# One attention-plus-rational-MLP kernel: scores in two 64-row halves of the array, a new task order, and 19 instead of 15 weight chunks converted in attention

## The chip, the core and the metric

The kernel runs on one core of one Trainium2 chip. The metric is the device time of one execution in microseconds (us). Each core has five engines that run their own instruction queues in order: PE (the matrix engine, with its weight loads shown as PEld), DVE (vector), ACT (scalar), POOL and SP. SP computes nothing here; it issues all the DMAs, in program order.

## The reference, cut to what matters

```python
# q, k, v: (4 batches, 12 heads, 448 tokens, 64) float32
scores = np.matmul(q, k.transpose(0, 1, 3, 2)) / 8.0
scores = np.where(np.triu(ones, k=1), -1e9, scores)        # causal
attn = np.exp(scores - scores.max(-1)); attn /= attn.sum(-1) + 1e-9
x = np.matmul(attn, v)                  # heads side by side: (1792, 768)
h = x @ w_in                            # w_in (768, 2048) float64
g = (a0 + a1*h + a2*h**2 + a3*h**3) / (1 + abs(b0)*abs(h) + abs(b1)*h**2 + 1e-6)
out = (g @ w_out).astype(np.float32)    # w_out (2048, 768) float64
```

## The kernel before, in words

**Attention** works on 24 pairs of heads (p = 0 to 23, `NP`). For a pair, q and k are loaded with one DMA for each head (`stage_load`, task `ld`), transposed on PE (`q`, `k`), and split into a high fp32r part on ACT (`qh`, `kh`) and the remainder on DVE (`ql`, `kl`). Scores (`s.i`, `stage_b_pe`) come in seven blocks of 64 queries. The stationary operand is `QH[p % 2][:, i]`: 128 columns, of which the first 64 hold head 0's queries in the upper 64 rows and the last 64 hold head 1's in the lower 64 rows, with zeros elsewhere. So a single matmul over all 128 rows gives both heads' scores, 64 output partitions each, over (i + 1) * 64 keys. Each block takes three passes (high times high, high times low, low times high); the two narrowest blocks do the first two in one instruction and add the result on DVE (`b`). DVE adds the mask and takes the row maximum (`m`), ACT takes the exponential (`e`), DVE the reciprocal of the sum (`r`), POOL multiplies (`n`). PE transposes the result in 16 pieces of 128 by 128, four to a PSUM tile (`c.0` to `c.3`). ACT (`a`) or DVE (`v`) copy these to SBUF. Four steps of plain fp32 matmuls multiply by v (`d.0` to `d.3`, `stage_d`), head 0 into output partitions 0 to 63 and head 1 into 64 to 127. For `d.3` the contraction has only 64 rows. ACT copies the result (`de`), and POOL splits it into `xh` and `xl` (`dh`, `dl`).

**Weight conversion.** The weights arrive as float64. A chunk (128 rows or columns of one weight, 768 KB) is turned into float32 by four steps (`conv_step`): step 0 on POOL for the first `NC` chunks and on ACT for the later ones, steps 1 to 3 on DVE (L146, L148, L153). The float32 chunk is stored to DRAM (`conv_store`, L159) and loaded again later (`load_w`, L172) into one of three buffers with the tag `ld`. There are 32 chunks. In attention, `cv.0` issues the POOL steps of a pair, `cv.1` and `cv.2` its DVE steps and `cv.3` the stores and the next loads. `quota(p)` is the number of DVE steps for a pair: three for the first two pairs, then two and one by turns, 39 in all, which is 13 chunks. Two more (13 and 14) are converted in `TAIL`, the other 17 in the MLP.

**Order.** `ORDER` is a list of tasks run for every pair p from 3 on; `@2` makes a task work on pair p - 2, `@-1` on pair p + 1. `HEAD` is a hand-over list for the first three pairs, `TAIL` the one that leads from the last pair into the MLP. The lists fix the order of the instructions on every engine and of the DMAs on SP.

**MLP.** 64 units t (4 token chunks of 512, 512, 384, 384 by 16 slices of the hidden width). `p1(t)` is 18 matmuls (L206), then ACT and DVE evaluate the rational function, and `p2(t)` is 24 or 18 matmuls (L520, L521). While the first token chunk is processed, the remaining 17 weight chunks are converted, one in each of t = 2 to 14 and a second one in t = 6, 8, 10 and 12 (`step`). `split_w` makes the high part on ACT (`w_hi`, L181) and the low part on POOL or DVE (`w_lo`, L189). At pair 22 four converted weights are loaded again, the fourth of which needs the buffer of the first to be free.

Of the kernel before, what the change touches and what calls it, by code (L numbers as in the profile page):

```python
# [24 lines left out]
NHEAD = 3  # L25
HEAD = """

ld@0 ab0 q@0 qh.0@0 xd.0 k@0 kh@0 ld@1 ql.0@0 qh.1@0 kl@0 xd.1 ql.1@0 s.1@0 s.0@0 s.2@0 b.1@0 b.0@0 m.0@0 q@1
m.1@0 e.0@0 cv.0@0 cv.1@0 qh.1@1 k@1 m.2@0 e.1@0 e.2@0 s.3@0 qh.0@1 ld@2 cv.2@0 s.6@0 s.4@0 ql.1@1 m.3@0 kh@1
e.3@0 kl@1 ql.0@1 s.5@0 m.6@0 e.6@0 m.5@0 cv.3@0 s.0@1 k@2 m.4@0 e.5@0 cv.0@1 cv.1@1 b.0@1 s.1@1 b.1@1 e.4@0  # L30
s.2@1 m.0@1 r@0 m.1@1 q@2 wh.0.0 n.4@0 e.0@1 n.1@0 s.6@1 m.2@1 e.1@1 e.2@1 n.0@0 n.5@0 qh.0@2 n.3@0 s.3@1 kh@2
n.6@0 qh.1@2 n.2@0 cv.2@1 m.6@1 ql.1@2 c.1@0 s.4@1 s.5@1 kl@2 a.1@0 m.3@1 e.6@1 ql.0@2 lv@0 c.0@0 m.5@1 e.3@1
s.1@2 ld@3 e.5@1 m.4@1 c.3@0 v.0@0 s.0@2 k@3 q@3 e.4@1 b.1@2 cv.3@1 r@1 cv.0@2 b.0@2 a.3@0 m.0@2 s.6@2 c.2@0
d.0@0 s.2@2 d.3@0 wl.0.0 m.1@2 cv.1@2 n.5@1 v.2@0 kh@3 wh.1.0 e.1@2 qh.1@3 e.0@2 d.1@0 m.2@2 m.6@2 s.3@2 kl@3
d.2@0 cv.2@2 n.2@1 n.4@1 m.3@2 n.6@1 n.0@1 n.1@1 e.6@2 c.1@1 cv.3@2 ld@4 s.4@2 qh.0@3 ql.1@3 s.5@2 lv@1 wl.1.0
# [13 lines left out]
def kernel(  # L49
# [11 lines left out]
    nc = tc.nc  # L61
# [15 lines left out]
    NC = 15  # L77
    NWB = (2, 3)
    NAB = 2
# [8 lines left out]
    mask = const.tile([P, S], F32, name="mask")  # L88
# [28 lines left out]
    def conv_load(m):  # L117
# [3 lines left out]
        early = m < NC or m % 2 == 0  # L121
# [11 lines left out]
    def conv_step(m, s):  # L133
# [9 lines left out]
        elif s == 1:  # L143
            pool = cv if m < NC or m % 2 == 0 else rp
# [71 lines left out]
    def stage_load(p):  # L216
        b, hp = divmod(p, HP)
        ts = {}
        for nm, src in (("q", q), ("k", k)):
            t = ld.tile([CP, NB, 2, D], F32, tag=nm, name=f"{nm}raw")  # L220
            for j in range(2):
                nc.sync.dma_start(
                    out=t[:, :, j], in_=src[b, 2 * hp + j].rearrange("(c p) d -> p c d", p=CP)
                )
            ts[nm] = t
        raw[p] = ts

    def stage_load_v(p):
        b, hp = divmod(p, HP)
        t = lv.tile([P, 2, 4, D], F32, tag="v", name="vraw")  # L230
# [7 lines left out]
        raw[p]["v"] = t  # L238


    def stage_a_pe(p, which):
        t = raw[p][which]
        ps = psa[p, which] = ps_t.tile([P, 512], F32, tag="t", name="psA")
        for c in range(NB):
            nc.tensor.transpose(  # L245
                ps[:, c * CP:(c + 1) * CP], t[:, c].rearrange("p j d -> p (j d)"), ident[:CP, :CP]
            )
# [4 lines left out]
    def q_pe(p):  # L252
        stage_a_pe(p, "q")


    def q_hi(p, j):
        nc.scalar.activation(
            out=QH[p % 2][half(j), :, j, :],
            in_=psa[p, "q"][half(j), :S].rearrange("d (i t) -> d i t", t=QB), func=AF.Copy, scale=SCALE,
        )  # L260

    def q_lo(p, j):
# [18 lines left out]

    def stage_b_pe(p, i):
        ps, w = ps_s.tile([P, 512], F32, tag="s", name="psS"), (i + 1) * QB
        pss[p, i] = ps
        qh, ql = (t[p % 2][:, i].rearrange("d j t -> d (j t)") for t in (QH, QL))
        if i < NAB:
            nc.tensor.matmul(
                ps[:, :2 * w].rearrange("m (x n) -> m x n", x=2), qh, K[p][:, :, :w], start=True, stop=True
            )
            nc.tensor.matmul(ps[:, :w], ql, K[p][:, 0, :w], start=False, stop=True, skip_group_check=True)  # L290
        else:
            for n, (a, b) in enumerate(((qh, 0), (qh, 1), (ql, 0))):
# [19 lines left out]
    def stage_b_exp(p, i):  # L312
        w = (i + 1) * QB
# [11 lines left out]
    def stage_b_norm(p, i):  # L325
        e = E[p % 2][i][:, :(i + 1) * QB]
# [5 lines left out]
    c_blocks = (  # L332
        [(0, 0), (0, 1), (0, 2), (0, 3)], [(0, 4), (0, 5), (0, 6), (3, 6)],
        [(1, 2), (1, 3), (1, 4), (1, 5)], [(1, 6), (2, 4), (2, 5), (2, 6)],
    )
    c_slot = (0, 8, 13, 7)

    def c_pe(p, n):
        ps = psc[p, n] = ps_t.tile([P, 512], F32, tag="t", name="psC")
        for o, (c, i) in enumerate(c_blocks[n]):  # L340
            nc.tensor.transpose(  # L341
                ps[:, o * P:(o + 1) * P], E[p % 2][i][:, c * P:(c + 1) * P], ident
            )
# [349 lines left out]
```

## Time and profile before

| what | value |
|---|---|
| time, three runs | 701.64 us median (701.62 to 702.39) |
| the profiled execution | 703.33 us, of which 701.6 us span from the first to the last instruction |
| granted PE clock, mean | 0.987 |
| busy, share of the span | PE 664.6 us (95%), DVE 541.1 (77%), ACT 441.0 (63%), POOL 198.7 (28%) |
| DMA | 161.98 MB, 231 GB/s, 72.4% of 16 engines |

Busy is the time in which an engine had at least one instruction in flight; ends of matmuls are modelled, so a PE that is busy all the time can still have gaps in its columns. The chain that ended last is 75% PE and 14% DVE.

### The profile page before, as it was taken

Reading aid. Unit: us, or ns where it says so; the run is one execution under the profiler, and the core shown is the slowest. Engines: PE = TensorE matmul, PEld = TensorE weight load, DVE = VectorE, ACT = ScalarE, POOL = GpSimd, SP = SyncE. Lnnn points to the kernel's source line nnn. Section 1 sums busy time; section 2 is a strip of 40 time slices with the busy share of each in tenths; the row PEclk is TensorE's granted clock in tenths of the full one; section 3 lists DMA queues with packets and bytes.
Section 4 is the critical chain, followed back from the end, with each engine's and each line's share of the span. In section 5 each row is a group of like instructions: output and inputs, shape, how many; then the busy total and the mean of one; then the engine's idle time right before and its main releaser. Section 6 shows DMA issues by size and latency. Waiting matters only on the chain.

```text
span 701.6 us, 11446 instructions
## 1 busy us (share of the span) xinstructions
PE 664.6 (95%) x3912; PEld 566.8 (81%) x3912; DVE 541.1 (77%) x1123; ACT 441.0 (63%) x962; POOL 198.7 (28%) x277
## 2 busy tenths in 40 slices
PE   5899999999968999888899999999999999999997
PEld 4687787787746787766688888888999999999996
DVE  4899999999829999999987766666566655666554
ACT  3789989989824676766567655554554454645543
POOL 4777887887837322122120000000000000000000
PEclk9999999999989999999999999999999999999999
DMA  8976788876433999887589766666877777877762
GB/s 195 214 161 147 178 191 183 170 162 147 149 113 108 358 349 346 284 268 253 191 316 359 275 226 242 247 220 214 282 273 254 257 244 257 304 264 241 255 225 112
DMA packets 110042, 161.98 MB, mean 231 GB/s; under 512 B 71072, under 2 KB 83360, under 8 KB 109984
## 3 DMA queue, kind: packets, MB, share of 16 engines
q1 hardware_dynamic: 109984, 161.25, 72.4%
q8 instruction: 31, 0.51, 0.3%
q14 instruction: 27, 0.22, 0.1%
HBM read 117.97 MB, written 43.25 MB: 230 GB/s over the span
## 4 chain that ended last, share of the span: by engine, by line
PE 75%; DVE 14%; issue 3%; DMA 3%; POOL 2%; ACT 1%; SPq 0%; DVEq 0%; POOLq 0%; ACTq 0%
PE psH L206 25%; PE psO L520 17%; PE psM L521 9%; PE psD L363 7%; PE psS L293 7%; PE psC L341 6%; PE psA L245 2%; DVE u L146 2%; DVE u L148 2%; DVE w L452 1%; DVE whl L189 1%; DVE p L483 1%; DVE p L460 1%; DMA raw<-in_moe_w_out_dram 1%; DVE p L477 1%
## 5 line engine op out<-in xcount | busy, mean ns | idle before, releaser
L206 PE MATMUL psH<-xh,whl 128*128 128x512 f32 (+1 forms) x768 | 177.7, 367 | 6.6 <-DVE p L460 6.6
L520 PE MATMUL psO<-whl,gh 128*128 128x512 f32 x448 | 160.3, 394 | 1.6 <-ACT gh L489 1.5
L206 PEld LDWEIGHTS psH<-xh,whl 128*128 128x128 f32 x768 | 136.5, 189 | 24.0 <-DVE p L460 5.5
L521 PE MATMUL psM<-whl,gh 128*128 128x256 f32 x448 | 126.2, 282 | 0.0
L327 POOL TENSOR_SCALAR e<-e,r 128x320 f32<-128x320 f32 (+6 forms) x168 | 94.2, 580 | 37.8 <-DVE nm L307 27.3
L467 ACT ACTIVATE u<-w,lnb 128x512 f32<-128x512 f32 (+1 forms) x64 | 43.0, 672 | 95.9 <-DVE w L452 95.9
L520 PEld LDWEIGHTS psO<-whl,gh 128*128 128x128 f32 x448 | 84.0, 187 | 22.1 <-ACT gh L489 5.1
L314 ACT ACTIVATE e<-psS,nm 128x64 f32<-128x64 f32 (+6 forms) x168 | 78.9, 474 | 23.1 <-DVE nm L307 20.4
L206 PE MATMUL psH<-xl,whl 128*128 128x512 f32 (+1 forms) x384 | 89.7, 369 | 0.0
L520 PE MATMUL psO<-whl,gl 128*128 128x512 f32 x224 | 81.2, 392 | 5.7 <-DVE gl L496 5.7
L496 DVE TENSOR_TENSOR gl<-p,gh 128x384 fp32r<-128x384 f32 (+1 forms) x62 | 38.4, 620 | 61.5 <-ACT gh L489 61.5
L521 PEld LDWEIGHTS psM<-whl,gh 128*128 128x128 f32 x448 | 84.5, 189 | 0.9
L206 PEld LDWEIGHTS psH<-xl,whl 128*128 128x128 f32 x384 | 71.8, 192 | 8.3
L445 ACT ACTIVATE u<-psH 128x512 f32<-128x512 f32 (+1 forms) x64 | 34.5, 538 | 69.1 <-PE psH L206 69.1
L521 PE MATMUL psM<-whl,gl 128*128 128x256 f32 x224 | 63.1, 282 | 0.0
L307 DVE CUSTOM_DVE_ANT_0 psS<-psS,mask 128x192 f32<-128x192 f32 (+4 forms) x120 | 56.9, 504 | 7.4 <-PE psS L293 7.2
L363 PE MATMUL psD<-at,vraw 128*64 128x448 f32 (+3 forms) x384 | 56.1, 408 | 6.7 <-DMA vraw<-in_v_dram 6.7
L293 PE MATMUL psS<-khl,qh 128*128 128x448 f32 (+4 forms) x240 | 60.8, 339 | 0.1
L341 PE MATMUL psC<-ident,e 128*128 128x128 f32 x384 | 56.1, 279 | 2.7 <-POOL e L327 2.7
L520 PEld LDWEIGHTS psO<-whl,gl 128*128 128x128 f32 x224 | 42.0, 188 | 15.4 <-DVE gl L496 6.7
L341 PEld LDWEIGHTS psC<-ident,e 128*128 128x128 f32 x384 | 43.1, 142 | 10.2 <-POOL e L327 5.7
L363 PEld LDWEIGHTS psD<-at,vraw 128*64 128x64 f32 (+1 forms) x384 | 21.6, 137 | 35.5 <-issue 24.3
(67 smaller groups left out, 1210.8 us busy)
## 6 DMA issues: line engine op xcount, KB each, us to landing
whl<-whl SPq DMA_DIRECT2D x112, 768.0 KB, 4.3
w<-w SPq DMA_DIRECT2D x34, 384.0 KB, 6.3
raw<-in_moe_w_in_dram SPq DMA_DIRECT2D x16, 768.0 KB, 6.2
w<-u SPq DMA_DIRECT2D x32, 384.0 KB, 2.8
raw<-in_moe_w_out_dram SPq DMA_DIRECT2D x16, 768.0 KB, 5.4
qraw<-in_q_dram SPq DMA_DIRECT2D x48, 112.0 KB, 4.7
kraw<-in_k_dram SPq DMA_DIRECT2D x48, 112.0 KB, 4.7
out_dram<-osb SPq DMA_DIRECT2D x14, 384.0 KB, 3.1
```

Source lines behind the costliest of these rows:

```text
L206: nc.tensor.matmul(ps, w[:, c * P:(c + 1) * P], x[c][:, lo:lo + n_tok], start=(c == 0 and n == 0), stop=(c == KD - 1 and n == 2),)
L293: nc.tensor.matmul(ps[:, :w], a, K[p][:, b, :w], start=(n == 0), stop=(n == 2))
L307: nc.vector.tensor_tensor_reduce(out=s, in0=s, in1=msk[p, i] if i < NAB else mask[:, S - w:], scale=-1.0, scalar=3e38, op0=ALU.add, op1=AL ...
L314: nc.scalar.activation(out=E[p % 2][i][:, :w], in_=pss[p, i][:, :w], func=AF.Exp, bias=nmx[p][:, i:i + 1], scale=-1.0, accum_out=SUM[p][:, ...
L327: nc.gpsimd.tensor_scalar(out=e, in0=e, scalar1=REC[p][:, i:i + 1], scalar2=0.0, op0=ALU.mult, op1=ALU.add)
L341: nc.tensor.transpose(ps[:, o * P:(o + 1) * P], E[p % 2][i][:, c * P:(c + 1) * P], ident)
L363: nc.tensor.matmul(ps[half(j), c * P:S], vt[:kk, j, c], AT[p][:kk, c_slot[c]:c_slot[c] + n, half(j)], start=(c == 0), stop=(c == 2), skip_ ...
L445: nc.scalar.activation(out=u, in_=h, func=AF.Abs)
L467: nc.scalar.activation(out=r, in_=w, func=AF.Ln, scale=2.0 ** -LSH, bias=lnb[:, 0:1])
L496: eng.tensor_tensor(out=gl, in0=pp, in1=gh.bitcast(F32), op=ALU.subtract)
L520: nc.tensor.matmul(acc[k], g, w[:, :512], start=first, stop=last)
L521: nc.tensor.matmul(m, g, w[:, 512:], start=first and k % 2 == 0, stop=last, skip_group_check=True)
```

## The change

Scores are taken in blocks of 128 queries. For the first 384 queries, head 0's operands lie in rows 0 to 63 and head 1's in rows 64 to 127, without zeros, and each head has its own matmul on its half of the rows, into its own PSUM bank. The last 64 queries keep the old form, with zeros (tile `Q6`, filled by DMA, zeroed once on POOL). There are seven row blocks with 128, 128, 256, 256, 384, 384 and 448 keys. The separate add of the narrow blocks is gone, `q_hi` and `q_lo` are one instruction each, q takes four DMAs instead of two, and `d.3` contracts over 128 rows (the unused ones zero). The tile for v is allocated once. The attention loop now starts at p = -2 with the ordinary order, and `HEAD` only loads. The order and the tail are new. `quota` is three steps for the first nine pairs and two for the others, 57 in all, which is 19 chunks; none is left for the tail, and 13 for the MLP, one in each of t = 2 to 14. The reload buffers (`ld` of `cv`) are four instead of three.

```diff
 ORDER = """
+e.0 m.1 m.2 e.1 v.0@2 cv.3 k@-1 n.0@1 ld@-2 n.4@1 m.3 lv@1 e.2 n.3@1 n.6@1 s.3 cv.2@-1 qh@-1 a.3@2 kh@-1 s.2
+n.2@1 n.1@1 d.0@2 e.3 m.6 m.4 d.3@2 n.5@1 e.6 m.5 e.4 ql@-1 d.1@2 d.2@2 cv.0@-2 de@2 c.2@1 e.5 kl@-1 c.1@1 dh@3
+cv.1@-2 s.0@-1 s.1@-1 a.2@1 c.0@1 m.0@-1 c.3@1 q@-2 r a.1@1 dl@3
 """
-NHEAD = 3
+NHEAD = -2
 HEAD = """
+ld@0 ab0 xd.0 ld@1 xd.1
 """
 TAIL = """
+v.0@2 n.0@1 n.4@1 lv@1 xr n.3@1 n.6@1 p1.0 wh.2.0 a.3@2 n.2@1 n.1@1 d.0@2 d.3@2 n.5@1 aa.0 d.1@2 d.2@2 xd.21 da.0
+de@2 c.2@1 c.1@1 dz.0 ab.0 dh@3 a.2@1 c.0@1 c.3@1 a.1@1 dl@3 p1.1 dh@2 aa.1 v.0@1 a.3@1 d.0@1 d.3@1 d.1@1 d.2@1 db.0 dy.0
+wl.2.0 lw.4.0 dl@2 da.1 gh.0 de@1 wh.0.1 p1.2 xl gl.0 dh@1 wl.0.1 dz.1 ab.1 wh.1.1 wh.3.0 xd.20 xd.22
+lw.2.1 wl.1.1 x.19.0 p2.0 lw.3.1 aa.2 lw.5.0 db.1 wl.3.0 dl@1 dy.1 wh.4.0 wl.4.0
 """
-    NC = 15
+    NC = 19
-            w = cv.tile([P, DM], F32, tag="ld", bufs=3, name="w")
+            w = cv.tile([P, DM], F32, tag="ld", bufs=4, name="w")
     def stage_load(p):
+        t = raw[p]["q"] = ld.tile([P, 3, 2, D], F32, tag="q", name="qraw")
+        for j in range(2):
+            src = q[b, 2 * hp + j]
+            nc.sync.dma_start(out=t[:, :, j], in_=src[:3 * P].rearrange("(c p) d -> p c d", p=P))
+            nc.sync.dma_start(out=Q6[p % 2][:, j, j], in_=src[3 * P:])
     def q_pe(p):
+        for c in range(3):
+            nc.tensor.transpose(
+                ps[:, c * P:(c + 1) * P], raw[p]["q"][:, c].rearrange("p j d -> p (j d)"), ident
+            )
+        for j in range(2):
+            nc.tensor.transpose(
+                ps[:, 3 * P + j * QB:3 * P + (j + 1) * QB], Q6[p % 2][:, j].rearrange("p j d -> p (j d)"),
+                ident[:QB, :QB],
+            )
     def stage_b_pe(p, i):
+        w = b_w[2 * i]
+        ps = [ps_s.tile([P, 512], F32, tag="s", name="psS") for _ in range(2 if i < 3 else 1)]
...
+        for n, (a, b) in enumerate(((QH, 0), (QH, 1), (QL, 0))):
+            for j in range(len(ps)):
+                d = half(j) if i < 3 else slice(None)
+                nc.tensor.matmul(
+                    ps[j][:, :w], a[p % 2][d, i * P:(i + 1) * P], K[p][d, b, :w],
+                    start=(n == 0), stop=(n == 2), skip_group_check=True,
+                )
-    def stage_b_add(p, i):
     def stage_d(p, c):
-                vt[:kk, j, c],
-                AT[p][:kk, c_slot[c]:c_slot[c] + n, half(j)],
+                ps[half(j), c * P:S], V[p % 2][:, j, c], AT[p, h][:, j, lo:lo + S - c * P],
     def quota(p):
-        return 3 if p < 2 else 2 - p % 2
+        return 3 if p < 9 else 2
         for p in range(NHEAD, NP):
+            if p in (0, 1):
+                split_w(p, 0)
-        step = {t: [todo.pop(0) for _ in range(1 + (t in (6, 8, 10, 12))) if todo] for t in range(2, NU)}
+        step = {t: [todo.pop(0) for _ in range(1) if todo] for t in range(2, NU)}
```

## Rows read from the trace of the kernel before

**Rows 1.** Windows: start:end, length, busy us of each engine, granted clock, DMA share, GB/s.

```profile
100.00:115.02 15.02, 15.02 (x122) 12.01 (x118) 14.12 (x49) 13.60 (x43) 12.08 (x20) 1.00 0.75 172
...
200.00:220.00 20.00, 14.83 (x77) 9.54 (x78) 9.87 (x14) 7.30 (x12) 8.40 (x9) 0.83 0.36 102
...
280.00:300.00 20.00, 17.32 (x85) 13.93 (x84) 19.93 (x26) 12.84 (x19) 4.14 (x2) 1.00 0.84 291
...
400.00:420.00 20.00, 20.00 (x105) 17.20 (x104) 12.37 (x18) 12.17 (x19) 0.00 (x0) 1.00 0.64 234
```

**Rows 2.** Chain that ended last, one pair: start us, us, engine, tile, line.

```profile
107.08 2.18 PE psD L363 x16
...
109.85 1.32 PE psS L293 x9
111.17 0.87 PE psC L341 x8
...
112.82 0.43 PE psA L245 x4
...
114.59 1.58 PE psD L363 x9
```

**Rows 3.** Groups by form on DVE, 40 to 180 us: busy us, mean ns | idle.

```profile
L263 DVE SCALAR_TENSOR_TENSOR ql<-psA,qh 64x448 fp32r<-64x448 f32 x38 | 23.6, 620 | 0.6
...
L153 DVE SCALAR_TENSOR_TENSOR u<-raw,u 128x768 uint32<-128x768 uint32 x10 | 12.5, 1248 | 0.0
L307 DVE CUSTOM_DVE_ANT_0 psS<-psS,mask 128x448 f32<-128x448 f32 x19 | 11.8, 620 | 0.0
...
L148 DVE SCALAR_TENSOR_TENSOR u<-raw,u 128x768 uint32<-128x768 uint32 x9 | 11.0, 1217 | 0.0
...
L307 DVE CUSTOM_DVE_ANT_0 psS<-psS,mask 128x256 f32<-128x256 f32 x19 | 8.2, 433 | 3.8 <-PE psS L293 3.7
...
L298 DVE TENSOR_TENSOR msk<-psS,mask 128x128 f32<-128x128 f32 x18 | 4.9, 273 | 0.0
L146 DVE TENSOR_SCALAR u<-raw 128x768 uint32<-128x768 uint32 x9 | 4.9, 543 | 0.0
...
L298 DVE TENSOR_TENSOR msk<-psS,mask 128x64 f32<-128x64 f32 x18 | 3.7, 207 | 0.0
```

**Rows 4.** Timeline of POOL and PE, start-up: start us, us, engine, line, instruction.

```profile
10.53 0.88 POOL L140 TENSOR_SCALAR raw<-raw 128x768 f32<-128x768 f32 x1 [3.29 <-DMA raw<-in_moe_w_in_dram]
...
30.56 0.97 PE L363 MATMUL psD<-at,vraw 128*64 128x448 f32 x4
...
39.46 2.25 PE L363 MATMUL psD<-at,vraw 128*64 128x448 f32 x16
```

**Rows 5.** From attention to MLP: timeline of PE and DVE, then chain.

```profile
188.83 2.25 PE L363 MATMUL psD<-at,vraw 128*64 128x448 f32 x16
...
196.91 1.52 PE L206 MATMUL psH<-xh,whl 128*128 128x512 f32 x6
205.17 4.12 PE L363 MATMUL psD<-at,vraw 128*64 128x448 f32 x16 [6.74 <-DMA vraw<-in_v_dram]
...
239.39 1.53 PE L206 MATMUL psH<-xh,whl 128*128 128x512 f32 x6
...
218.73 3.40 DVE L146 TENSOR_SCALAR u<-raw 128x768 uint32<-128x768 uint32 x2
...
201.22 0.32 SPq L172
...
201.63 3.40 DMA vraw<-in_v_dram
...
222.66 6.77 DMA raw<-in_moe_w_out_dram
```

**Rows 6.** Timeline of PE: first six matmuls of p1(8), p1(9), p1(10).

```profile
272.70 1.66 PE L206 MATMUL psH<-xh,whl 128*128 128x512 f32 x6
...
284.30 1.65 PE L206 MATMUL psH<-xh,whl 128*128 128x512 f32 x6 [0.73 <-DVE p L460]
...
292.98 1.56 PE L206 MATMUL psH<-xh,whl 128*128 128x512 f32 x6
```

More of the change, by code (lines that the diff above doesn't have):

```diff
@@ L87 @@
     ident = const.tile([P, P], F32, name="ident")
-    mask = const.tile([P, S], F32, name="mask")
+    mask = const.tile([P, 3 * P + S], F32, name="mask")
     ab = const.tile([P, 6], F32, name="ab")
@@ L216, in stage_load @@
     def stage_load(p):
+        if p in raw:
+            return
         b, hp = divmod(p, HP)
[L218 to L226, printed above, removed]
+        raw[p] = {}
+        t = raw[p]["q"] = ld.tile([P, 3, 2, D], F32, tag="q", name="qraw")
[3 more added lines that the diff above has]
+            nc.sync.dma_start(out=Q6[p % 2][:, j, j], in_=src[3 * P:])
+        t = raw[p]["k"] = ld.tile([CP, NB, 2, D], F32, tag="k", name="kraw")
+        for j in range(2):
+            nc.sync.dma_start(
+                out=t[:, :, j], in_=k[b, 2 * hp + j].rearrange("(c p) d -> p c d", p=CP)
+            )
     def stage_load_v(p):
         b, hp = divmod(p, HP)
-        t = lv.tile([P, 2, 4, D], F32, tag="v", name="vraw")
+        t = V[p % 2]
         for j in range(2):
@@ L237, in stage_load_v @@
         )
[L238 to L247, printed above, removed]
     def half(j):
@@ L252, in q_pe, with q_hi, q_lo @@
     def q_pe(p):
[L253 to L262, printed above, removed]
+        ps = psa[p, "q"] = ps_t.tile([P, 512], F32, tag="t", name="psA")
+        for c in range(3):
+            nc.tensor.transpose(
+                ps[:, c * P:(c + 1) * P], raw[p]["q"][:, c].rearrange("p j d -> p (j d)"), ident
+            )
+        for j in range(2):
+            nc.tensor.transpose(
+                ps[:, 3 * P + j * QB:3 * P + (j + 1) * QB], Q6[p % 2][:, j].rearrange("p j d -> p (j d)"),
+                ident[:QB, :QB],
+            )
+    def q_hi(p):
+        nc.scalar.activation(out=QH[p % 2], in_=psa[p, "q"], func=AF.Copy, scale=SCALE)
+    def q_lo(p):
         nc.vector.scalar_tensor_tensor(
-            out=QL[p % 2][half(j), :, j, :],
-            in0=psa[p, "q"][half(j), :S].rearrange("d (i t) -> d i t", t=QB), scalar=SCALE,
-            in1=QH[p % 2][half(j), :, j, :].bitcast(F32), op0=ALU.mult, op1=ALU.subtract,
+            out=QL[p % 2], in0=psa[p, "q"], scalar=SCALE, in1=QH[p % 2].bitcast(F32),
+            op0=ALU.mult, op1=ALU.subtract,
         )
     def k_pe(p):
-        stage_a_pe(p, "k")
+        ps = psa[p, "k"] = ps_t.tile([P, 512], F32, tag="t", name="psA")
+        for c in range(NB):
+            nc.tensor.transpose(
+                ps[:, c * CP:(c + 1) * CP], raw[p]["k"][:, c].rearrange("p j d -> p (j d)"), ident[:CP, :CP]
+            )
     def k_hi(p):
@@ L329, in stage_b_norm @@
         )
[L332 to L334 removed]
+    c_parts = (
+        [(0, 0, 0), (P, 0, 1)], [(0, 0, 2), (P, 0, 3), (P + QB, 3, 3)],
+        [(0, 1, 1), (P, 1, 2)], [(0, 1, 3), (QB, 2, 2), (QB + P, 2, 3)],
     )
[L336 removed]
+    c_of = {0: (0, 0), 3: (0, S), 1: (1, 0), 2: (1, S - P)}
     def c_pe(p, n):
[L339 to L343, printed above, removed]
+        ps = psc[p, n] = ps_t.tile([P, 2, 256], F32, tag="t", name="psC")
+        for o, c, i in c_parts[n]:
+            keys = slice(c * P, (c + 1) * P)
+            if i == 3:
+                nc.tensor.transpose(
+                    ps[:, :, o:o + QB], E[p % 2][6][:, keys], ident.rearrange("p (j t) -> p j t", j=2)
+                )
+            else:
+                for j in range(2):
+                    nc.tensor.transpose(ps[:, j, o:o + P], E[p % 2][2 * i + j][:, keys], ident)
     def c_ev(p, n, eng):
[L346 to L348 removed]
+        h = n // 2
+        if (p, h) not in AT:
+            AT[p, h] = at.tile([P, 2, 512], F32, tag=f"at{h}", name="at")
+        o = AT[p, h][:, :, (n % 2) * 256:(n % 2 + 1) * 256]
         ps = psc.pop((p, n))
```

90 lines of the change are left out of this document (33 added, 57 removed).

## The prediction

> **What bounds the kernel now.** I read the windows first, then the chain, then the groups by form and timelines. The windows [rows 1] show four regimes. In attention PE is busy 15.02 of 15.02 us at clock 1.00, with DVE at 14.12 close behind, then ACT 13.60 and POOL 12.08. At 200 to 220 no engine is full: PE has 14.83 of 20 and the clock drops to 0.83. At 280 to 300 DVE is full (19.93) and PE has room. From 400 on PE is full again and stays so to the end.
>
> The chain [rows 2] confirms the first: from one pair's first v matmul (107.08) to the next's (114.59) it holds PE pieces alone. A pair costs 7.51 us and PE sets it. DVE's 7.06 us a pair (14.12 / 2) is the next limit. In the transition [rows 5] PE does p1(0) until 198.43, then waits 6.74 us until 205.17 for a v tile. The chain names the cause: the v DMA starts right behind a DMA of L172 at 201.22, the fourth weight reload, which finds three buffers taken and holds SP's queue until POOL has finished with the first. A second transfer, raw chunk 15, starts late at 222.66 and takes 6.77 us, with ACT standing in front of it. DVE also does leftover conversion there (218.73). In the DVE-bound stretch [rows 6], p1(9) follows p1(8) by 11.6 us and p1(10) follows p1(9) by 8.7: the units after a doubled conversion are the long ones.
>
> **PE in attention.** Rates from [rows 2]: nine score passes of 256, 384 and 320 columns take 1.32 us, 0.458 ns a column, so 0.117, 0.176 and (448) 0.205 us a pass. Eight 128-column transposes take 0.87, 0.109 each; a score pass of 192 columns or fewer I price at the same 0.11, because its 128-column weight load is as long. Scores before: 3 x (0.205 + 0.176 + 0.147 + 0.117 + 0.11) + 4 x 0.11 = 2.70 us. After, if the two halves of the rows run at the same time, each pair of passes costs one: 3 x (0.11 + 0.117 + 0.176) + 3 x 0.205 = 1.82. Gain 0.88. If they run one after the other, 6 x 0.403 + 0.615 = 3.03, a loss of 0.33.
>
> No row shows two halves of the rows. The nearest is the v step: 16 fp32 instructions into two halves of the columns take 2.18 us [rows 2], while their 4,096 columns at the transposes' 0.85 ns (also fp32) would take 3.48 in sequence and 1.74 in parallel. So column halves do overlap, and I take the parallel price for row halves.
>
> The rest, 2.18 - 1.74 = 0.44 us, belongs to four changes of the array's shape in that step (to 128 by 64, to 64 by 64 for d.3, back, and out): 0.11 each. The change takes d.3's two away, but adds entry and exit: full to row halves (s.2), to column halves (d), to full (c.2), to row halves (s.0, s.1), to full (c.0), to row halves (the two 64-row transposes of q), to full. Seven instead of four: +0.33; bounds 0 (if row halves switch free) and 0.33. The transposes of q go from four of 112 (0.43) to five: 5 x 0.109 = 0.55, +0.12. Sum: 7.51 - 0.88 + 0.33 + 0.12 = 7.08.
>
> The Trainium skill, "TensorEngine Tiling (Array Packing)", section Key Properties, says that changing the tiling mode drains the engine, which speaks against a change that adds modes; the 0.11 us that the trace gives agrees. "TensorE: Matmul & The Clock Gate", Part 3, Measured speedup vs the span model, gives 3.07x for four row tiles; scaled to two tiles, an estimate of 1.53x, the three blocks would cost 2.42 / 1.53 = 1.58 instead of 1.21 us, and the whole time would be 680.
>
> **DVE in attention** [rows 3]. The adds go (0.273 + 0.207 = 0.48). Two ql of 0.620 become one of 512 columns, about 0.69: -0.55. The maxima get 192 more columns at (620 - 433) / 192 = 0.97 ns: +0.19. A chunk's three steps cost 0.543 + 1.217 + 1.248 = 3.01 us, 1.00 a step; 1.5 steps a pair become 3 and then 2. So 7.06 - 0.84 + 1.5 = 7.72 early and 7.06 - 0.84 + 0.5 = 6.72 later. Early pairs are then bound by DVE, later ones by PE. With some friction I take 7.8 and 7.2. The loop runs pair p's steps one or two iterations ahead, so six intervals between first v matmuls are early (pairs 0 to 6) and fourteen late.
>
> Edits at nothing: ACT has 6.80 us a pair, loses half a microsecond with one qh instead of two, and gains wider exponentials; POOL has 6.04 [rows 1], gains 0.5 at most for one POOL step every pair and 0.2 to 0.7 for wider products. Both lie under 7.8; if POOL's worst came, the late pairs would wait at most some 0.1 us. The two more q DMAs a pair carry no more bytes. DMA share is 0.75 over 7.51 us, 5.6 us a pair with half a chunk (0.58 MB of 1.29). Another half costs 2.5 us at the pair's mean rate, or 1.7 at the rate of 280 to 300 (291 GB/s at share 0.84): 7.3 to 8.1. At the upper end, six early pairs lose 0.3 each. The row masks, memsets and v tile are under POOL's start.
>
> **Start-up.** The plain order puts three DVE steps of chunk 0 ahead of the first ql. Chunk 0 was on POOL at 10.53 [rows 4]; its DMA is now two issues later, at about 0.5 each: 11.5, POOL 0.9, DVE 3.0, then ql and kl 1.2, scores: the first full iteration begins near 17. Two iterations of 7.7 and the 1.9 us of k and s.3, s.2 ahead of the v step put pair 0's first v matmul at 34.5 (before: 30.56), and pair 1's at 42 instead of 39.46. Bounds 32 and 37.
>
> Pair 21's comes at 34.5 + 6 x 7.8 + 14 x 7.2 + 6.1 (the last interval lacks the next pairs' k and q) = 188.2, against 188.83: -0.6. Attention is a draw, with six more chunks converted in it.
>
> **Transition.** From there to p1(4) it was 50.56 us (188.83 to 239.39). The fourth buffer lets SP pass, v is loaded ahead, the conversions of chunks 13 and 14 are gone, and chunk 19's load lands inside attention. PE's own sequence is then v 2.0, 16 transposes 1.8, p1 4.3, v 2.0, transposes 1.8, p1 4.3, v 2.0, p1 4.3, p2 4.1, p1 4.3, p2 4.1, and 2.3 us of wait for the last copy, which the new tail puts behind p1(1)'s three ACT passes: 37.3. Gain 13.3; bounds 6.6 (the late v alone) and 16.
>
> **MLP.** Four doubled units become single: 11.6 - 8.7 = 2.9 us each [rows 6], 11.6 in all. From p1(16) on PE is the bound, as in the 400 row [rows 1], and nothing changes. Sum: 0.6 + 13.3 + 11.6 = 25.5; 701.6 of span gives **676**. The profiled execution's 703.33 is 1.7 above its span, but the median of the runs, 701.64, stands at the span, so 676 is the forecast for the median.
>
> **The rivals.**
> - *Weight loads of the two halves come one after the other* (0.22 us a pass): scores 3 x 3 x 0.22 + 0.62 = 2.6, PE 7.86. Six early pairs +0.1, fourteen +0.7: **687**. Against it: the column halves' overlap.
> - *Row halves run one after the other*: PE 8.3; 6 x 0.5 + 14 x 1.1 and 1 for the rest: **695**. The change then doesn't do what it says and is carried by the tail and the MLP.
> - *Friction*: two engines above 93%, so late pairs at 7.6, or half of the transition's stall comes back as a wait on POOL's low parts: **683 to 689**.
> - *Slower*: halves one after the other, and each weight load exposed because it may not pass a matmul in its own half. Then 6 x (0.11 x 3 + 0.055 + 0.117 + 0.176) + 0.62 = 4.7, PE 9.95: 6 x 2.2 + 14 x 2.8 = 52, **728**. It decides from 8.65 us a pair on (25.5 gained back over 20 pairs). Against it: today's full-height passes run at column rate, so their loads are hidden [rows 2].
> - *No change*: about 8.6 us a pair by a mix; nothing in the rows points there.
>
> **How the numbers follow.** Forecast 0.60 (own range 667 to 685: free shape changes 14 x 0.35 = 5, start and tail 2 each; up: DMA 2, the transition's lower bound 7), loads in sequence 0.12, halves in sequence 0.10, friction 0.10, slower 0.06, no change 0.02. The range 665 to 696 holds the first four but for their edges. Faster by over 0.2% (about what a measurement of this kernel can tell from no change) 0.91, within it 0.02, slower 0.07.
>
> **What would show it.** The chain in attention after pair 8 should be PE at 7.1 to 7.3 us a pair, with DVE full before that at 7.7 to 7.9; paired score matmuls should start within 10 ns of each other; no wait on the v DMA ahead of pair 22's v step, p1(4) near 226; p1 intervals of 8.3 to 8.6 up to p1(15). A pair above 7.8 late in attention, or ACT waiting on a raw chunk in the transition, would make me wrong.

## The result and the profile after

The changed kernel takes 683.47 us (median of four runs, 682.85 to 686.28) beside 702.01 for the kernel before (four runs, 701.62 to 703.56). The ratio is 0.974, with a 95% interval of 0.971 to 0.977. The forecast was 676, with a range of 665 to 696. The profiled execution has a span of 681.6 us, 20.0 less than before, where the working had 25.5 less. Repeats on two other chips gave a ratio of 0.980 (0.977 to 0.982) and of 0.973 (0.971 to 0.974). The first of these is the odd one: its median is 688.49 us, and the experiments come back to that.

The windows of the changed kernel come first, with the columns of [rows 1]: two early pairs, two late pairs, the transition, then the two MLP stretches of [rows 1].

```profile
63.59:79.86 16.27, 14.96 (x126) 10.39 (x124) 15.33 (x45) 12.98 (x41) 15.22 (x21) 1.00 0.87 226
102.56:117.10 14.54, 14.54 (x126) 10.37 (x124) 13.63 (x43) 13.29 (x43) 13.93 (x21) 1.00 0.84 215
196.30:232.85 36.55, 34.77 (x202) 27.08 (x202) 21.81 (x29) 22.58 (x42) 22.35 (x25) 1.00 0.50 163
280.00:300.00 20.00, 20.00 (x103) 16.55 (x102) 20.00 (x26) 14.50 (x22) 6.95 (x3) 1.00 0.92 323
400.00:420.00 20.00, 20.00 (x102) 17.08 (x101) 14.44 (x22) 10.52 (x16) 0.00 (x0) 1.00 0.67 238
```

The early pairs take 8.14 us each, and no engine is quite full: DVE has 15.33 of 16.27, POOL 15.22. In the late pairs PE is full at 7.27 us a pair, against 7.51 before. POOL has gone from 12.08 [rows 1] to 13.93 for two pairs, and the DMA share from 0.75 to 0.84. In the MLP at 280 PE is now full beside DVE.

The chain that ended last, through one late pair of the changed kernel (start us, us, what):

```profile
102.63 1.88 PE psD L359 x16
...
105.53 0.88 PE psS L284 x12
...
107.77 0.27 PE psA L242 x2
108.03 0.53 PE psA L259 x4
108.56 1.34 PE psS L284 x9
109.90 1.28 PE psD L359 x9
```

As in [rows 2] there are PE pieces alone. The scores take 2.22 us (0.88 + 1.34), the v step 1.88.

The timeline of PE in the transition, and of the first matmuls of p1(8), p1(9) and p1(10), as in [rows 5] and [rows 6]:

```profile
196.30 1.95 PE L359 MATMUL psD<-at,vraw 128*64 128x448 f32 x16
199.91 1.63 PE L194 MATMUL psH<-xh,whl 128*128 128x512 f32 x6
204.19 1.09 PE L359 MATMUL psD<-at,vraw 128*64 128x448 f32 x8
...
215.17 1.08 PE L359 MATMUL psD<-at,vraw 128*64 128x320 f32 x8 [1.39 <-ACT at L349]
...
232.85 1.53 PE L194 MATMUL psH<-xh,whl 128*128 128x512 f32 x6
...
266.29 1.65 PE L194 MATMUL psH<-xh,whl 128*128 128x512 f32 x6
...
274.81 1.64 PE L194 MATMUL psH<-xh,whl 128*128 128x512 f32 x6
...
283.33 1.65 PE L194 MATMUL psH<-xh,whl 128*128 128x512 f32 x6
```

Pair 22's v step (204.19) follows p1(0) at once; the wait of 6.74 us in [rows 5] is gone. The largest wait left is 1.39 us, in pair 23's v step. From pair 21's v step to p1(4) it is 36.55 us (before 50.56), and p1(8), p1(9) and p1(10) follow each other by 8.52.

The start-up of the changed kernel (timeline of POOL, DVE and PE):

```profile
17.29 1.83 POOL L177 TENSOR_TENSOR whl<-u,whl 128x768 fp32r<-128x768 f32 x1
...
26.21 1.82 POOL L177 TENSOR_TENSOR whl<-u,whl 128x768 fp32r<-128x768 f32 x1 [2.84 <-DVE u L134]
28.39 4.76 POOL L317 TENSOR_SCALAR e<-e,r 128x128 f32<-128x128 f32 x7 [0.37 <-DVE r L313]
...
17.37 2.17 DVE L134 TENSOR_SCALAR u<-raw 128x768 uint32<-128x768 uint32 x1
...
26.58 1.47 DVE L312 TENSOR_SCALAR sums<-sums 128x7 f32<-128x7 f32 x1
...
17.43 0.47 PE L284 MATMUL psS<-khl,qh 64*128 64x128 f32 x2 [5.29 <-DVE khl L268]
25.78 0.33 PE L284 MATMUL psS<-khl,qh 64*128 64x128 f32 x2 [1.42 <-DVE khl L268]
34.47 0.69 PE L284 MATMUL psS<-khl,qh 64*128 64x128 f32 x4
39.90 1.95 PE L359 MATMUL psD<-at,vraw 128*64 128x448 f32 x16
```

Pair 0's v step comes at 39.90, against 30.56 in [rows 4]. The three first scores are those of pairs 0, 1 and 2. Two instructions of DVE stand out, the 2.17 us of L134 and the 1.47 us of L312. Each begins while POOL makes the low part of a weight chunk (L177).

### The profile page after: what moved, and what is told of

The parts are those of the page before. It is cut to its first block, busy times and chain, and to the rows that moved or that the text cites. A ratio compares the mean times of both kernels' runs of the same rounds, so it can differ in the third digit from the quotient of the medians.

```text
span 681.6 us, 11741 instructions
## 1 busy us (share of the span) xinstructions
PE 654.2 (96%) x3984; PEld 544.7 (80%) x3984; DVE 521.6 (77%) x1044; ACT 434.0 (64%) x941; POOL 212.0 (31%) x274
## 4 chain that ended last, share of the span: by engine, by line
PE 90%; DMA 3%; DVE 2%; POOL 2%; issue 1%; ACT 1%; SPq 1%; DVEq 0%; POOLq 0%
PE psH L194 34%; PE psO L515 23%; PE psM L516 12%; PE psS L284 7%; PE psC L340 5%; PE psD L359 5%; PE psA L259 1%; PE psC L335 1%; DMA vraw<-in_v_dram 1%; POOL e L317 1%; DVE psS L297 1%; DMA raw<-in_moe_w_in_dram 1%; PE psA L238 1%; DMA raw<-in_moe_w_out_dram 1%; PE psA L242 1%
## 5 line engine op out<-in xcount | busy, mean ns | idle before, releaser
L317 POOL TENSOR_SCALAR e<-e,r 128x128 f32<-128x128 f32 (+3 forms) x168 | 99.4, 610 | 18.2 <-PE psC L340 7.9
L304 ACT ACTIVATE e<-psS,nm 128x128 f32<-128x128 f32 (+3 forms) x168 | 83.6, 505 | 22.8 <-DVE nm L297 14.8
L194 PE MATMUL psH<-xl,whl 128*128 128x512 f32 (+1 forms) x384 | 87.5, 362 | 0.0
L440 ACT ACTIVATE u<-psH 128x512 f32<-128x512 f32 (+1 forms) x64 | 34.5, 539 | 70.9 <-PE psH L194 70.9
L297 DVE CUSTOM_DVE_ANT_0 psS<-psS,mask 128x128 f32<-128x128 f32 (+3 forms) x168 | 73.2, 466 | 8.3 <-PE psS L284 8.1
L284 PE MATMUL psS<-khl,qh 64*128 64x128 f32 (+3 forms) x336 | 54.3, 356 | 11.8 <-DVE khl L268 6.7
L469 DVE SCALAR_TENSOR_TENSOR w<-w,u 128x512 f32<-128x512 f32 (+1 forms) x64 | 41.3, 645 | 17.7 <-ACT u L465 17.7
L484 ACT CAST gh<-p 128x512 fp32r<-128x512 f32 (+1 forms) x64 | 36.7, 574 | 25.1 <-DVE p L478 25.1
L340 PE MATMUL psC<-ident,e 128*128 128x128 f32 x288 | 47.0, 287 | 4.4 <-DVE ql L251 3.2
L284 PEld LDWEIGHTS psS<-khl,qh 64*128 64x128 f32 (+1 forms) x336 | 31.2, 198 | 24.2 <-DVE khl L268 7.0
L447 DVE SCALAR_TENSOR_TENSOR w<-w,bb,u 128x512 f32<-128x512 f32 (+1 forms) x64 | 44.4, 694 | 7.1 <-ACT w L441 7.1
```

The costliest lines, as they stand in the source:

```text
L194: nc.tensor.matmul(ps, w[:, c * P:(c + 1) * P], x[c][:, lo:lo + n_tok], start=(c == 0 and n == 0), stop=(c == KD - 1 and n == 2),)
L284: nc.tensor.matmul(ps[j][:, :w], a[p % 2][d, i * P:(i + 1) * P], K[p][d, b, :w], start=(n == 0), stop=(n == 2), skip_group_check=True,)
L297: nc.vector.tensor_tensor_reduce(out=s, in0=s, in1=m, scale=-1.0, scalar=3e38, op0=ALU.add, op1=ALU.min, accum_out=nmx[p][:, i:i + 1],)
L304: nc.scalar.activation(out=E[p % 2][i][:, :w], in_=pss[p, i][:, :w], func=AF.Exp, bias=nmx[p][:, i:i + 1], scale=-1.0, accum_out=SUM[p][:, ...
L317: nc.gpsimd.tensor_scalar(out=e, in0=e, scalar1=REC[p][:, i:i + 1], scalar2=0.0, op0=ALU.mult, op1=ALU.add)
L340: nc.tensor.transpose(ps[:, j, o:o + P], E[p % 2][2 * i + j][:, keys], ident)
```

## The experiments

Each set of runs was made on another chip, so the time of the changed kernel in the same set stands beside a result where there is one. The set with the other order, three buffers, 15 chunks and the spread steps has none; there the run with the other order (684.28) is the nearest to it. Ratios are to the kernel before in the same set. "Interval" is the time from one pair's first v matmul to the next pair's.

### Do the two halves of the rows really run at the same time?

First, the order: head 0's three passes, then head 1's.

```diff
-        for n, (a, b) in enumerate(((QH, 0), (QH, 1), (QL, 0))):
-            for j in range(len(ps)):
+        for j in range(len(ps)):
+            for n, (a, b) in enumerate(((QH, 0), (QH, 1), (QL, 0))):
```

> Scores head by head: three passes on the upper half of the rows, then three on the lower, so that at most the passes at the seams overlap. Theory (the two halves work at the same time, and that pays for the change): twelve narrow passes of s.0 and s.1 take 9 slots instead of 6, the six of s.2 five instead of three: late pairs 7.27 + 0.34 + 0.35 = 7.95, early ones 8.2 to 8.7, the time 10 to 14 us more, 693 to 697. Rival (the weight loads or DVE hide the order): late pairs under 7.5, at most 3 us more.

684.28 us, ratio 0.974 (0.972 to 0.975); late intervals 7.29, but for one of 7.99. The order costs 0.02 us a pair, so the expected loss was wrong. The single records of one 128-key block show why (start us, distance to the record before in ns, weight):

```
106.536    0  qh        head by head
106.546   10  qh
106.700  154  qh
106.709    9  qh
106.812  103  ql
106.822   10  ql
105.462    -  qh        the changed kernel, heads by turns
105.465    3  qh
105.625  160  qh
105.628    3  qh
105.738  110  ql
105.742    4  ql
```

The program issues qh, qh, ql for one head and then the same for the other, yet the records run by pairs. The records do not name the half. But the second weight load waits for the same semaphore as the first, as a head's first pass does, and the third for another one, as a second pass does in the changed kernel. So the second record is read as the other head's first pass: it starts 10 ns after one for the first half, ahead of passes that were issued before it.

Second, the halves taken away: the same instructions over all 128 rows. The two heads' scores are summed by this, so these three blocks' output means nothing; sizes and counts stay.

```diff
-                d = half(j) if i < 3 else slice(None)
+                d = slice(None)
```

> The score passes of the three blocks with two heads each run over all 128 rows, one after the other, instead of over half the rows each (the two heads' scores are summed, so the output is left wrong); number, columns and order of the instructions stay. Theory (row halves run at the same time, and a change of the array's shape costs 0.11 us): a late pair costs 7.27 + 3 x (0.11 + 0.117 + 0.176) - 3 x 0.11 = 8.15 us; 14 late pairs +12, six early ones +2: about 697 us. First rival (changes of shape cost nothing): 8.48 a pair, +17 and +3, 703 us. Second rival (the halves gain nothing, the pass was bound by something else): 7.3 a pair, as the changed kernel.

695.56 us, ratio 0.989 (0.987 to 0.990), beside 683.95 for the changed kernel. Late intervals are 7.97, nearly all of them exactly. The chain of a late pair:

```profile
116.85 1.39 PE psS L284 x12
118.24 0.44 PE psC L340 x4
...
120.24 1.68 PE psS L284 x9
```

At full height the passes cost what the prediction's prices say: 6 x (0.11 + 0.117) = 1.36 for the first piece (1.39) and 6 x 0.176 + 3 x 0.205 = 1.67 for the second (1.68). In row halves the columns are worth half of the paired ones, 0.68 and 1.14, but the changed kernel's pieces took 0.88 and 1.34, and its transposes behind them 0.59 instead of 0.44. So halving gains 1.21 us of columns and gives back 0.51 to 0.55. If all of that is the three changes of shape that the full height does without, each costs 0.17 to 0.18 us, not 0.11.

### The tail and the MLP

Back to three reload buffers. The low part of one more weight had to move from the later line of the tail into its first, so that the buffer comes free.

```diff
-            w = cv.tile([P, DM], F32, tag="ld", bufs=4, name="w")
+            w = cv.tile([P, DM], F32, tag="ld", bufs=3, name="w")
-... n.6@1 p1.0 wh.2.0 a.3@2 ...
+... n.6@1 p1.0 wh.2.0 wl.2.0 a.3@2 ...
```

> Three reload buffers instead of four, and in the tail POOL's low part of that first weight right behind its high part, without which the three could not be waited for. Theory (the old stall of 6.74 us was SP's queue held by the fourth reload): PE waits for pair 22's v again, 5 to 8 us ahead of its v step, and the time is 5 to 7 us more, 689 to 690. Rival (the new order of the tail hides it): no such wait over 2 us, the time within 1.5 us of 683.5.

695.72 us, ratio 0.990 (0.988 to 0.992). From pair 21's v step to p1(4) it is 45.8 us instead of 36.55. The timeline of SP, then of PE:

```profile
189.71 19.34 SPq L160 DMA_DIRECT2D w<-w  x4
...
209.62 1.24 SPq L224 DMA_DIRECT2D vraw<-in_v_dram  x2
...
213.89 3.78 PE L359 MATMUL psD<-at,vraw 128*64 128x448 f32 x16 [7.93 <-DMA vraw<-in_v_dram]
```

This is the stall of [rows 5] again: the four reloads hold SP's queue from 189.71 until POOL has freed a buffer, and the v load behind them is issued only at 209.62. With the order of the tail that it allows, the fourth buffer is worth 9.3 us in this stretch, and 9.9 to 11.4 us of the time beside the two runs of this set that have it and as many chunks (685.80 and 684.28). How much of that is the moved low part was not tried.

Back to 15 chunks in attention and four doubled units in the MLP:

```diff
-    NC = 19
+    NC = 15
-        return 3 if p < 9 else 2
+        return 3 if p < 2 else 2 if p < 19 else 1
-        step = {... range(1) if todo] ...}
+        step = {... range(1 + (t in (6, 8, 10, 12))) if todo] ...}
```

> Only 15 chunks converted in attention (three steps for pairs 0 and 1, two up to 18, one after), and again a second one in units 6, 8, 10 and 12 of the MLP; all else as changed. Theory (conversion moved into attention is paid there only where DVE is over PE): early pairs 7.3 instead of 8.0, 5 us less in attention, 13 more in the MLP: 8 us more, 691 to 692. Rival (the MLP's gain came from elsewhere): within 2 us of 683.5.

693.99 us, ratio 0.988 (0.986 to 0.989). From p1(4) to p1(16) it is 114.24 us instead of 101.6; the four doubled units take 11.68, 11.16, 11.51 and 10.85, the rest 8.25 to 9.3. Two of the first matmuls, before and after a doubled unit:

```profile
265.85 1.64 PE L194 MATMUL psH<-xh,whl 128*128 128x512 f32 x6
...
277.53 2.20 PE L194 MATMUL psH<-xh,whl 128*128 128x512 f32 x6
```

Pair 21's v step comes at 195.75, against 198.2 and 198.0 in the two runs of this set that keep 19 chunks in the same pairs (196.30 in the first profile). The early intervals fall to between 7.27 and 7.75, so it is the third step that makes them 8.1, but four of the late ones grow to between 7.7 and 9.7. Converting four more chunks in attention costs it 0.5 to 2.5 us and saves the MLP 12.6.

### The start-up and the early pairs

The first two weight chunks are split late: reloads in pairs 6 and 8, split in pairs 10 and 12.

```diff
-            if p in (0, 1):
-                split_w(p, 0)
+            if p in (6, 8):
+                load_w(p // 2 - 3, 0)
+            if p in (10, 12):
+                split_w(p // 2 - 5, 0)
```

> The two weight splits that the loop makes at pairs 0 and 1 are made at pairs 10 and 12, from the stored weights. Theory (the start is late because POOL's two low parts stretch DVE's work, 2.17 instead of 0.55 us and 1.47 instead of 0.17, and hold the products back): pair 0's first v matmul at 36 to 37.5 instead of 39.9, the time 3 us less, 680 to 681. Rival (the start is late only because chunk 0's conversion stands ahead of the first ql): 39.5, the time within 1 us of 683.5.

691.67 us, ratio 0.985 (0.981 to 0.989), beside 688.49 for the changed kernel. DVE in the start-up (timeline) has lost both long instructions:

```profile
17.25 0.56 DVE L134 TENSOR_SCALAR u<-raw 128x768 uint32<-128x768 uint32 x1
...
26.71 0.17 DVE L312 TENSOR_SCALAR sums<-sums 128x7 f32<-128x7 f32 x1
```

So POOL's L177 is what stretches them, 0.56 to 2.17 us and 0.17 to 1.47. Yet pair 0's v step comes only 1.1 us earlier (38.36 beside 39.48), and it lies anywhere between 39.48 and 41.34 in the seven profiles whose edits do not move the start's work. The interval of pair 10 becomes 11.84. POOL there (timeline):

```profile
114.52 1.44 POOL L128 TENSOR_SCALAR raw<-raw 128x768 f32<-128x768 f32 x1 [1.02 <-DMA raw<-in_moe_w_in_dram]
...
117.66 2.24 POOL L177 TENSOR_TENSOR whl<-w,whl 128x768 fp32r<-128x768 f32 x1
119.88 4.17 POOL L317 TENSOR_SCALAR e<-e,r 128x128 f32<-128x128 f32 x7
```

POOL has 6.97 of 7.27 us busy in a late pair, so 2.24 more find no room: the chain there runs from the late raw chunk (1.02 us of wait) through POOL's work, this L177 included, to PE. How much of the 4.6 us is the split's own is not shown, since the changed kernel of this set has 11.03 at the same pair without it (below). The first split falls into an interval of 9.01 whose chain waits for a load of k.

The same with the conversion tasks put behind the first pair's own tasks in the iteration p = -1:

```diff
-            attend(p, plan)
+            attend(p, plan if p != -1 else sorted(plan, key=lambda x: x[0] is conv))
```

> As the run with the late splits, and in the iteration before pair 0 the conversion steps come behind the score work on DVE. Theory (both matter; DVE's whole work in the first iterations stays, so only what it idles is won): pair 0's first v matmul 1.5 to 3 us earlier than with the late splits alone, 34 to 35, the time 678 to 679.5. Rival (DVE's work bounds the start anyway): less than 0.7 us earlier than with the late splits alone.

690.39 us, ratio 0.982 (0.978 to 0.985). Pair 0's v step comes at 35.40, 3.0 us before that of the late split alone, as expected. But pair 6's comes at 88.17, where the changed kernel has 88.23 in this set: the intervals of the early pairs are 7.89 to 10.83. The chain in the longest waits for a raw chunk:

```profile
65.19 8.60 DMA raw<-in_moe_w_in_dram
...
73.87 0.89 POOL raw L128
```

This earlier start gains nothing that lasts. That the chunks' loads set the pace is read from this chain; no run brings the loads forward.

The three-step pairs spread over the whole of attention instead of the first nine:

```diff
-        return 3 if p < 9 else 2
+        return 3 if p in (0, 1, 4, 7, 10, 13, 16, 19, 22) else 2
```

> The nine pairs with three conversion steps are 0, 1, 4, 7, 10, 13, 16, 19 and 22 instead of 0 to 8; 57 steps as before. Theory (a pair with three steps costs 8.14 because DVE's 7.7 us and the wait between ql and the transposes add up within the pair, but a neighbour with two has room): half of the excess goes, 2 to 4 us less, 680 to 681. Rival (nothing carries over from pair to pair): every pair with three steps still takes 8.1, the time within 1 us of 683.5.

685.80 us, ratio 0.975 (0.973 to 0.977). Pair 21 comes at 200.79, not earlier. Most of the pairs with three steps take 8.2 to 9.0 us singly, no less than the 8.14 of a row of them, and POOL waits 13.5 us for raw chunks in attention (0.6 in the first profile). Whether nothing carries over to a neighbour, or these waits use it up, is not separated.

### The late pairs

The last 64 queries of both heads brought over by one transpose of 128 rows instead of two of 64, which also takes away one change of shape in and one out:

```diff
-        for j in range(2):
-            nc.tensor.transpose(ps[:, 3 * P + j * QB:...], Q6[p % 2][:, j]..., ident[:QB, :QB])
+        nc.tensor.transpose(ps[:, 3 * P:], Q6[p % 2].rearrange("p j d -> p (j d)"), ident)
```

> The last 64 queries of both heads lie in one tile of 128 rows, so q takes one full transpose instead of two on 64 rows: two changes of the array's shape and one transpose less in each pair. Theory (a change costs about 0.1 us and PE sets the late pairs): late pairs at 6.95 to 7.05 instead of 7.27, 4 to 5 us less in all, 679. Rival (DVE with its 6.8 us and the waits between DVE and PE set the late pairs): 7.15 or more, at most 2 us less. Rival (row halves switch free): late pairs at 7.15, 2 us less.

687.13 us, ratio 0.978 (0.975 to 0.982), beside 688.49. Undisturbed late intervals are 6.98, and the piece in the chain is

```profile
154.10 0.11 PE psA L241
154.21 0.38 PE psA L255 x4
```

instead of 0.27 and 0.53: 0.29 us a pair saved. Less the one transpose (0.11), that leaves 0.09 for each of the two changes of shape, half the price that the run at full height gives. Six of the fourteen late intervals, though, lie between 7.3 and 9.3, and the gain is lost in them: the two ratios are the same within their intervals.

### Long pairs

The changed kernel again, in the set of the late split, the moved conversion tasks and the one transpose:

> The changed kernel itself, once more, as the reference for the runs beside it. Both theories: 683.5 us, within 1.5.

688.49 us, ratio 0.980 (0.977 to 0.982). This is 5 us more than in the first set, and 3.5 more than the expectation allows. The profiled execution was the slowest of the five (691.74). Its profile is nearly all as the first one, except that two late intervals are 11.03 and 11.34 instead of 7.27, 7.8 us in all. The chain in the second, then the waits around the first and around the second, then windows of the second (the wait, and what comes behind it):

```profile
165.25 6.94 DMA qraw<-in_q_dram
172.28 0.52 PE psA L238 x3
```

```profile
PE psA L238 <- DMA qraw<-in_q_dram: 1.5, 1, 1.5
```

```profile
PE psA L238 <- DMA qraw<-in_q_dram: 1.7, 1, 1.7
```

```profile
168.00:172.20 4.20, 2.56 (x25) 2.02 (x25) 3.53 (x13) 2.71 (x10) 3.69 (x6) 1.00 0.66 122
172.20:176.40 4.20, 4.10 (x18) 2.90 (x18) 1.41 (x3) 2.20 (x6) 4.12 (x7) 0.59 0.41 93
```

The transposes of q wait for a load that is still under way 7 us after its issue, and PE is busy only 2.56 of 4.20 us. In the next 4.2 us its granted clock is 0.59: the three q transposes take 0.52 instead of 0.33. The wait (1.7 us, and 0.4 of idle time just ahead of it) costs about 2 us and the clock behind it, by an estimate, 4.2 x 0.41 = 1.7, about 3.7 of the 4.1 us. Long pairs of the late split and of the version with three edits (below) show the same fall, with a mean clock of 0.76 and 0.74 over the 7.0 and 6.5 us behind the gap, though it is POOL that PE waits for there. Pairs of 8.7 and 9.3 in the run with one transpose, whose longest gap is 1.1 us, keep a clock of 1.00. To test the late load as the cause, q and k of pair p + 3 are loaded in pair p, a pair earlier, into the same buffers:

```diff
-... k@-1 n.0@1 ld@-2 n.4@1 ...
+... k@-1 n.0@1 ld@-2 le@-3 n.4@1 ...
+        "le": lambda p: p > 2 and stage_load(p),
```

> The changed kernel itself, for comparison with the three beside it. Theory (in attention the q and k loads, queued behind raw chunks, land with almost no margin, so that a transfer a little late holds a pair up): 683 to 689 us with a spread of 3 us or more between its runs, and in the profile up to three late pairs of 8 to 12 us, each with a wait of a transpose for the q or k DMA; the others at 7.27. Rival (the long pairs come from POOL, whose raw chunk lands late): long pairs with a wait of POOL on the raw chunk instead.

> The q and k of pair p + 3 are loaded in pair p, one pair earlier than in the changed kernel, into the same buffers; nothing else moves. Theory (late q and k loads make the long pairs): no transpose waits for a q or k DMA, late pairs 7.27 with none above 7.8, attention's last v step (pair 21) at 194.5 to 197.5, total 681 to 684 with a spread under 2 us. Rival (DMA has no room left, its share is 0.84 to 0.91, so whatever goes first makes the next late): waits of POOL for raw chunks take their place, as many long pairs as beside it, total as the changed kernel's within 1 us.

The changed kernel takes 683.95 us here, ratio 0.973 (0.971 to 0.974), with one late interval of 7.81 and the rest at 7.27 to 7.35: none of the long pairs came back. The early load takes 689.57, ratio 0.980 (0.978 to 0.982): 5.6 us slower. The waits in attention (40 to 205 us), first of the changed kernel, then of the early load:

```profile
POOL raw L128 <- DMA raw<-in_moe_w_in_dram: 2.2, 3, 1.2
```

```profile
POOL raw L128 <- DMA raw<-in_moe_w_in_dram: 6.4, 4, 2.4
POOL raw L128 <- DMA raw<-in_moe_w_out_dram: 2.8, 2, 2.0
```

No transpose waits for q or k any more, and no late interval is above 9.3. POOL waits for the raw chunks instead, 9.2 us in place of 2.2; two early intervals are 9.0, and the last of the late ones is 9.22. That is the rival's mechanism: here the order of the loads decided who was late, not whether anyone was. The loss is larger than the rival's 1 us, and part of it is a start 1.4 us later, whose cause is open.

Last, three edits put together: the early load, the one transpose, and a late split, now in pairs 13 and 16 and with DVE for the low part. Only the split is shown here:

```diff
+            if p in (11, 14):
+                load_w((p - 11) // 3, 0)
+            if p in (13, 16):
+                split_w((p - 13) // 3, 0)
-        eng = nc.gpsimd if t < 3 or n == 1 else nc.vector
+        eng = nc.vector if t < 2 and n == 0 else nc.gpsimd if t < 3 or n == 1 else nc.vector
```

> Three edits together: q and k loaded a pair earlier; the last 64 queries of both heads brought over by one transpose of 128 rows instead of two of 64; the high and low parts of the first two weight chunks made in pairs 13 and 16 of attention (low part on DVE, from a reload) instead of in pairs 0 and 1. Theory: start 1 to 1.5 us earlier, late pairs 6.98 with none above 7.8 but the two that hold the split (about 7.5): 677 to 680 us. Rival (work put into a late pair, or the reload's 0.4 MB, holds it up as it did with POOL): pairs of 8 us and more around 11 to 16, 682 to 686 us.

688.34 us, ratio 0.980 (0.977 to 0.983), so slower than the changed kernel. The profiled execution was the slowest of six (695.10). Pair 0's v step comes at 35.85, 4.6 us earlier, but pair 6's at 88.94, and late intervals of 8.5, 10.6, 8.9 and 10.7 stand among those of 6.98. Ahead of the second of these POOL waits for a chunk, and PE then for POOL's products:

```profile
138.61 0.91 POOL L128 TENSOR_SCALAR raw<-raw 128x768 f32<-128x768 f32 x1 [2.29 <-DMA raw<-in_moe_w_in_dram]
```

No version here beats the changed kernel by more than its spread.

## Why the prediction was right, and where it was not

The sign and the places of the gain were right: all of it lies in the transition and the MLP, and attention, forecast as a draw, loses. By terms, on the span: attention was forecast at -0.6 and came out at +7.5; the transition at -13.3 and came out at -14.0; the MLP at -11.6 and came out at -13.8. With 0.4 more after p1(16) that makes -19.9. So attention missed by 8.1 us, and the total is within 7.5 us of the forecast only because the transition and the MLP, better than forecast by 0.7 and 2.2, made up for part of it; that they did is luck. The time alone would also fit the friction rival (683 to 689), but neither of its conditions came: late pairs are at 7.27 and not 7.6, and no stall on POOL's low parts is left in the transition. One of the prediction's own signs of being wrong, a late pair above 7.8, is absent from the first profile, but the set at 688.5 has it twice. What the new order of tasks is worth by itself was not tried.

**Row halves.** Right. They run at the same time, their matmuls start 2 to 5 ns apart, and full height shows the loss that they avoid (0.70 us a pair). The two rivals in sequence (687, 695) and the slower one (728) needed late pairs of 7.86 and more; 7.27 was measured. The Trainium skill, "TensorE: Matmul & The Clock Gate", Part 3, Measured speedup vs the span model, gives 3.07 times for four row tiles. The 1.53 for two is the prediction's own scaling of that, an estimate, and it was too low: pairs of 384-column passes follow each other by 0.174 us, as single passes do at full height, so the columns cost half, 1.21 us of 2.42.

**The price of a shape change.** The mechanism was right and the size too small for score passes: 0.11 us from a residue of the v step, against 0.17 to 0.18 by the run at full height. Three changes at 0.06 to 0.07 more each make 7.08 into 7.26 to 7.29; 7.27 was measured. That the sum comes out so well is partly luck: the changes around the transposes of q cost 0.09 by the run with one transpose, and the score pieces of the kernel before add up to 2.59 us in its chain, not to the 2.70 that the working priced, so the price seems to depend on which pieces meet, and no more than 0.09 to 0.18 us is shown. The Trainium skill, "TensorEngine Tiling (Array Packing)", Key Properties, says that changing the tiling mode drains the engine, and these prices agree with that.

**Start-up.** This is the term that failed: 34.5 forecast, 39.90 measured, 5.4 of the 8.1 us by which attention missed. The first scores came when forecast (17.43). The time from a pair's first scores to the v step ahead of the next was taken as 1.9 us; a late pair's chain has 4.37 (105.53 to 109.90), and here it took 5.43. That is 2.5 miscounted, and 1.1 more that no run explains (in the repeat it took 6.06). The two iterations took 8.35 and 8.69 instead of 7.7. POOL's two L177 held up DVE in both, but with the late split they took 8.43 and 7.67: only the second became shorter, and what makes the first long stays open. The note that POOL's work lies "under POOL's start" was wrong in that it left DVE out. The 4 us that the runs at 35.40 and 35.85 gain at the start are given back by pair 6, though (the late split alone keeps its 1 us until then), so the start was not the only limit either.

**Early pairs.** 7.8 forecast, 8.02 on average measured, +1.3 in all. DVE's work was sized rightly (7.67 a pair by the windows, forecast 7.72). The waits from 55 to 90 us show the coupling that the step lacked:

```profile
ACT e L304 <- DVE nm L297: 5.4, 8, 1.2
...
PE psC L340 <- DVE ql L251: 2.6, 4, 0.7
DVE psS L297 <- PE psS L284: 1.6, 4, 0.4
```

PE waits for DVE's `ql` to give back a PSUM buffer before it can transpose and go on to the next scores, and then DVE waits for those: 0.4 us a pair in which the bound engine stands still.

**Late pairs and DMA.** 7.2 forecast, 7.28 measured, +1.1. The step took DMA as a mean (7.3 to 8.1 us a pair at full use). The mean share is 0.78 over the late pairs (88 to 190 us) and 0.89 ahead of them, and the runs show what that does not: a load for which PE waits 1.5 to 1.7 us held up a pair by 3.8 to 4.1, since the gap in PE was followed by a lower clock as well. The profile in the set at 688.5 had two such pairs, those of the two other sets none or one of half a microsecond; why the loads were later there stays open.

**Transition and MLP.** The causes were right, as the runs with three buffers and with doubled units show, and both stretches came out a little better. In the transition the wait for the last copy was forecast at 2.3 us and took 1.39. A single unit takes 8.53 instead of the 8.7 that was carried over from [rows 6], since with one chunk a unit the chain holds PE pieces alone; and the unit before p1(16), 9.96 before, fell to 8.51, which the working had left out. p1(4) came at 232.85 and not near 226 for attention's sake alone.

## What to carry to other kernels

Splitting the array's rows between two heads gained half the columns here and paid 0.1 to 0.2 us for each change of shape, so put pieces of one shape side by side and count the changes. Work that is moved out of a bound stretch into a nearly full one is free only while the queues behind it (POOL, DMA) still have room: in this attention, with a DMA share of 0.78 to 0.89, loading q and k earlier changed who waited and gained nothing. When a start-up is costed, measure the whole distance from first scores to first result in a steady iteration, and then ask whether the loads behind it would let it go any faster.

## What was not expected of the hardware

- Matmuls on different halves of the rows, as the records are read, ran in pairs 9 to 11 ns apart although three passes of one half were issued ahead of the other's, and the order cost 0.02 us a pair.
- A DVE instruction on 7 columns took 1.47 us instead of 0.17 while a two-input instruction of POOL was running; the Trainium skill, "SBUF — State Buffer", section SBUF: two separate sides, says that some DVE instructions share a port pair with POOL, which one of the two holds for a whole instruction while the other waits. The runs agree: the 1.47 us end at 28.05 and POOL's instruction at 28.03, and with the split moved away the same instruction takes 0.17.
- A single gap of 1.7 us in a PE that is otherwise full was followed by 4.2 us at a mean granted clock of 0.59, mostly at the lower of the two levels (1.2 GHz is 0.50, 2.4 GHz is 1.00), so that the gap cost about twice its length. Gaps of at most 1.1 us, 1.7 in a pair of 9.3, left it at 1.00 in the run with one transpose. Between 25 and 35 us of the changed kernel the clock was 0.66 and 0.50; in the repeat it stayed at 1.00 there, and pair 0's v step came no earlier (40.47 beside 39.90). PE waits for other engines in that stretch, and no cost of the lower clock shows.
